# Four edits around the end of a kernel's first matrix product: who computes the last pair's moments, where its sums stand in the order, and when the weights' splitting begins

## The chip, the cores and the metric

The kernel runs on one core of a Trainium2 chip. The metric is the device time of one launch in microseconds (us), taken as the median of the runs shown. The kernel before took 2634.07 us (three runs, 2632.92 to 2637.14).

## What is computed

Two layers, each of a Fourier mixing step and a two-matrix network, over x with 2048 rows (S) and 576 columns (D); the network's inner width is 4608 (F).

```python
def _A_ref(x, dft_seq_re, dft_seq_im, dft_hid_re, dft_hid_im):
    a = jnp.einsum("bsd,ed->bse", x, dft_hid_re)
    b = jnp.einsum("bsd,ed->bse", x, dft_hid_im)
    return jnp.einsum("ts,bse->bte", dft_seq_re, a) - jnp.einsum("ts,bse->bte", dft_seq_im, b)

def _B_ref(x, w1, b1, w2, b2):
    y = _layernorm(x, axis=-1)
    h = _gelu(jnp.einsum("bsd,df->bsf", y, w1) + b1)
    return jnp.einsum("bsf,fd->bsd", h, w2) + b2

x = A_x
x = x + _A_ref(_layernorm(x), ...)
x = x + _B_ref(_layernorm(x), ...)
x = x + _A_ref(_layernorm(x), ...)
x = x + _B_ref(_layernorm(x), ...)
```

All data are float32.

## The kernel before

**Arithmetic.** A float32 product is made of three matmuls in a shorter format: each operand is split into a high part (ScalarE copies it into the rounded format) and a low part (VectorE subtracts the high part from the value), and TensorE adds high·high, high·low and low·high (`PASSES`). Most products also go through a scheme with seven instead of eight block products (numbers 1 to 7 in `ORDER`), so blocks are added and subtracted before they are split, and products are added to each other after (the "posts", done by VectorE, ScalarE and GpSimd).

**Stages of a layer.** First the sequence transform (class `Sequence`): it multiplies x, normalized, by the DFT matrix over rows. The 2048 rows are eight pairs (p = 0 to 7) of two 128-row tiles. Output tiles 0 and 1 (`PLAIN`) use plain products, pair by pair as the pairs come in (`first_mms`). Output tiles 2 to 15 use the seven products (`mms`), 24 matmuls each, so one output tile is 168 matmuls. Then follow, for each half of the rows, the hidden transform (`Hidden`, `hidden`) and the network (`mlp`). The network runs in groups g = 0 to 8 of two inner chunks q = 2g and 2g+1: an inner chunk is seven products of seven matmuls (49), each followed by a post, and between the chunks stand the second matrix's products of the group before (96 and 72 matmuls).

**The order of the work is written out by hand**: each engine does its instructions in the order in which the program issues them, and waits for what they need. Three orders matter here.

- `fill` prepares the pairs. For each pair: moments of the rows (`norm_stats`, which calls `stats_of_pair`), normalizing on ScalarE (`normalize`), high parts (`high_z`), low parts (`low_z`, VectorE), the sums of the seven-product scheme (`right_sums`: one subtraction on VectorE, then two on GpSimd, into the one buffer `t`), their high parts (`high_sums`, ScalarE) and low parts (`low_sums`, VectorE). At its end it also prepares the first left blocks of output tile 2: `low(*self.steps[0], True)` is the low part for product (2, 1) and, with it, three sums of the tile's blocks, `steps[1]` is product (2, 6), `steps[2]` is (2, 2). For pair p > 2 the four small steps behind the moments (L246, L247, L251, L252: add epsilon, power −1/2, multiply by the mean, negate) all stand on GpSimd.
- `run` walks the products n = 0, 1, ... (n = 0 to 6 is output tile 2): low part of product n+2, high part of n+3, the 24 matmuls, the post, and then two calls of `pump`.
- `pump` takes one step of `weights()`, a background generator that splits the network's first matrix into parts in DRAM, once for the whole program. It has 18 chunks of seven splits. It takes 4 steps for its first loads, one for the first high part, and two per split: the first makes the low part (VectorE, 128x384), a GpSimd sum if the split has one, and the next split's high part (ScalarE, L282 and L283); the second (`keep`) stores the split and loads a raw block for the next chunk. The last `keep` is step 257, and the last of chunk q is step 2·(7q + 6) + 7. A split lies in one of three buffers, so a high part waits until the store of three splits ago has landed. Pumps come from `run` (two per product, except product 2 of each tile: 84 of the 98 products, 168 pumps) and from the network's first half (12 per group from group 1 on, at the slots in `BEHIND`). If a chunk is wanted that isn't made yet, `load_w` pumps until it is (`while made[0] <= q`), in one go, at the place where it stands.

In the network, chunk q+1 is first wanted at the fourth product of chunk q (product 5), ahead of that product's matmuls and post. The post of product 5 is one VectorE addition that reads the bank into which product 3, two products on, adds; product 7 lies between.

Of the kernel before, what the change touches and what calls it, by code (L numbers as in the profile page):

```python
# [18 lines left out]
NP = NT // 2  # L19
# [139 lines left out]
def spectral_mixer(ctx: ExitStack, tc: tile.TileContext, x, dh, c0, cs, w1, b1, w2, b2, out):  # L159
# [35 lines left out]
    def add(engine, dst, a, b, op=OP.add):  # L195
        engine.tensor_tensor(dst, a, b, op=op)  # L196
# [65 lines left out]
    def weights():  # L262
        b = raw(4, 3 * P)
        a22, a21, a11, a12 = (b[:, k] for k in range(4))
        g = nc.gpsimd
        steps = ((4, a22, lambda: add(g, a22, a21, a22)), (1, a11, lambda: sub(g, a21, a11, a21)),
                 (5, a22, lambda: sub(g, a11, a22, a11)), (2, a12, lambda: sub(g, a12, a12, a11)),
                 (7, a21, None), (6, a11, None), (3, a12, None))

        def load(q, k):  # L270
            if q < NQ:
                dma(b[:, k], w1[q][:, k])

        def at(n):
            return stage(3, 5 * P)[:, n % 3]

        def cut(a):
            return a.rearrange("p (k f) -> p k f", f=P)

        def high(n):  # L280
            src, t = cut(steps[n % 7][1]), cut(at(n))
            nc.scalar.activation(t[:, 1:4:2], src[:, 0:3:2], AF.Copy)  # L282
            nc.scalar.activation(t[:, 2], src[:, 1], AF.Identity, bias=power[:, 2:3], scale=middle)  # L283

        def low(n):

            q, k = divmod(n, 7)
            i, src, then = steps[k]
            t = cut(at(n))
            sub(nc.vector, t[:, 0:5:2], cut(src), t[:, 1:4].bitcast(F32))  # L290
            if then:
                then()

        def keep(n):

            q, k = divmod(n, 7)
            stores[0].dma_start(w1s[q, steps[k][0] - 1], at(n).bitcast(F32))
            if k in (2, 4, 5, 6):
                load(q + 1, (2, 4, 5, 6).index(k))
            if k == 6:  # L300
                made[0] = q + 1

        for k in range(4):
            load(0, k)
        for _ in range(4):
            yield
        high(0)
        for n in range(7 * NQ):
            yield
            low(n)  # L310
            if n + 1 < 7 * NQ:
                high(n + 1)
            yield
            keep(n)
        stage.free()
        raw.free()
# [11 lines left out]
    class Sequence:  # L328
        def __init__(self, src, early):

            self.src, self.early = src, early
            self.Z, self.parts, self.b12, self.v, self.x, self.mv = [None] * NP, {}, {}, {}, {}, {}
            self.ready, self.closed, self.wish = 0, False, list(range(NP))
            self.normal, self.begun, self.xs, self.before = set(), {}, [], self.prepare()
            self.pieces = self.fill()


# [31 lines left out]
        def fill(self):  # L369
# [49 lines left out]
            for p in range(NP):  # L419
                if p in (1, 2) and self.early:  # L420
                    self.load_left(p + 1)
                if p + 1 < NP:
                    if p == 2 and self.early:
                        while self.closed:
                            yield
                        self.own.idle.insert(0, R.place(OWN_AT + 6 * NP * P + 2 * Z_N, 2 * NP * P))
                        sums, *self.xs = [A.alloc(2 * D, low=True) for _ in range(5)]
                    self.load_some()
                    while not self.has_z(p + 1):
                        yield  # L430
                if p == 1 and self.early:

                    self.high_sums(0)
                    self.low_left(1)
                    yield
                    self.low_sums(0)
                    yield
                    self.low_z(1)
                    yield
                    self.right_sums(1)  # L440
                    yield
                if p == 0 and not self.early:
                    self.half_stats(1)
                    self.low_z(0)
                    self.norm_stats(1)
                    self.low_left(0)
                    yield
                if p == 1 and not self.early:
                    self.low_left(1)
                if p + 1 < NP:  # L450
                    self.norm_stats(p + 1)
                if p == 0 and not self.early:
                    self.right_sums(0)
                    self.load_some()
                if p and (p != 1 or not self.early):
                    self.high_sums(p - 1)
                if p == 3 and self.early:

                    self.low_sums(p - 1)
                    self.t = sums  # L460
                    assert self.has_left(1)
                    for k in range(4, NP):
                        self.load_left(k)
                if p == 0 and self.early:
                    self.high_left(1)
                    self.high_z(1)
                elif p + 1 < NP:
                    self.high_parts(p + 1)
                yield
                if p > 1:  # L470
                    self.low_left(p)
                if p == 3:
                    self.begin_loads()
                if p == NP - 1:
                    self.idle += self.ring[4:]
                    self.high(PLAIN, 1)
                if p > 1 or p and not self.early:
                    yield
                    self.low_z(p)
                if p and (p not in (1, 3) or not self.early):  # L480
                    self.low_sums(p - 1)
                if p == NP - 1:
                    yield
                elif p > 1 or p and not self.early:
                    self.right_sums(p)
                    yield
            self.low(*self.steps[0], True)
            self.high(*self.steps[1])
            self.right_sums(NP - 1)
            self.high(*self.steps[2])  # L490
            self.high_sums(NP - 1)
            self.low(*self.steps[1])
            self.low_sums(NP - 1)
            yield
            for b in self.xs:
                if b.at != raw.at or self.early:
# [40 lines left out]
        def norm_stats(self, p):  # L537
            if p not in self.mv:
                halves = range(2 if p in self.begun else 0, 4)
                st, mv = self.begun.pop(p, None) or moments()  # L540
                measure(self.x[p], st, halves)
                self.mv[p] = stats_of_pair(st, mv, p == 0 and not self.early, p > 2, p == 1 and not self.early)

        def normalize(self, p):
            for h in range(2):
                at = slice(2 * h, 2 * h + 2)
                if p == 0 and not self.early:
                    v, mv = self.x[p][:, at], self.mv[p][:, h]
                    nc.vector.tensor_scalar(v, v, mv[:, 0:1], mv[:, 3:4], op0=OP.subtract, op1=OP.mult)
                    continue  # L550
                if p == 1 and not self.early:
                    shift(self.mv[p][:, h])
                normalize(self.x[p][:, at], self.x[p][:, at], self.mv[p][:, h])

# [168 lines left out]
        def run(self, hidden):  # L723
# [12 lines left out]
            for n, (t, i) in enumerate(steps):  # L736
                self.load_c()
                if n + 2 < len(steps):
                    self.low(*steps[n + 2])
                if i == 2 and t + 1 < NT:  # L740
                    self.sums(t + 1)
                self.load_c()
                if n + 3 < len(steps):
                    self.high(*steps[n + 3])
                self.mms(t, i)
                self.post(t, i)
                if n == 1:
                    self.first_turn(0, outs[0])
                    hidden.reserve()
                    self.first_post(1, outs[1])  # L750
                if n == 3:
                    self.first_turn(1, outs[1])
                if t == NT - 1:
                    hidden.begin(self, ORDER.index(i))
                if n == 3 and not self.early:
                    dma(b1t, b1)
                if n % 3 == 2 and 8 <= n < 8 + 3 * KH and not self.early:
                    dma(dhd[n // 3 - 2], dh[n // 3 - 2])
                if i != 2:
                    pump()  # L760
                    pump()
            for k in range(2):
# [709 lines left out]
```

## Time and profile before

| | us |
|---|---|
| median of three runs | 2634.07 |
| the profiled execution | 2634.11 |
| its span in the profile | 2632.3 |
| TensorE busy (99%) | 2617.2 |
| VectorE busy (70%) | 1834.1 |
| ScalarE busy (42%) | 1118.3 |
| GpSimd busy (30%) | 796.7 |

In the profile PE is TensorE's matmul, PEld its weight load, DVE VectorE, ACT ScalarE, POOL GpSimd and SP the engine that issues most DMAs. A group's line is that of the helper which issues it: L209 is every matmul, L196 an addition, L199 a subtraction (so low parts stand there, as R<-A,R), L667 the high part of a left block, L598 `high_sums`, L569 and L571 `high_z`, L256 `normalize`, L236 `shift`, L282 and L283 the high parts of a weights' split, L700 to L714 posts of the sequence transform. Times in a timeline are us from the start of the span; the number behind a group's x is how many instructions it merges; brackets give the engine's idle time before it and what ended it. Output tile 2 of the first layer runs from about 62 to 89 us, tile 3 to about 111 us, the first half of the first network from about 441 to 875 us, and the second layer's sequence transform from about 1300 us.

### The profile page before, as it was taken

Reading aid. Unit: us, or ns where it says so; the run is one execution under the profiler, and the core shown is the slowest. Engines: PE = TensorE matmul, PEld = TensorE weight load, DVE = VectorE, ACT = ScalarE, POOL = GpSimd, SP = SyncE. Lnnn points to the kernel's source line nnn. Section 1 sums busy time; section 2 is a strip of 40 time slices with the busy share of each in tenths; the row PEclk is TensorE's granted clock in tenths of the full one; section 3 lists DMA queues with packets and bytes.
Section 4 is the critical chain, followed back from the end, with each engine's and each line's share of the span. In section 5 each row is a group of like instructions: output and inputs, shape, how many; then the busy total and the mean of one; then the engine's idle time right before and its main releaser. Section 6 shows DMA issues by size and latency. Waiting matters only on the chain. (4 is left out here: it accounts for less than half of the span.)

```text
span 2632.3 us, 44772 instructions
## 1 busy us (share of the span) xinstructions
PE 2617.2 (99%) x17252; PEld 2466.4 (94%) x17252; DVE 1834.1 (70%) x2574; ACT 1118.3 (42%) x1815; POOL 796.7 (30%) x644
## 2 busy tenths in 40 slices
PE   9999999999999999999999999999999999999999
PEld 9999999899999989998999999999999999899998
DVE  8999987878777665556687776576555557655555
ACT  6555555555453443333354333353333325433332
POOL 6333433534444332222251000132222233322222
PEclk9999999999999999999999999999999999999999
DMA  5687786788788666677554333746666685666664
GB/s 184 226 273 241 244 259 215 262 276 286 275 286 299 184 194 195 195 222 212 170 177 132 124 123 124 210 153 192 195 195 195 195 274 157 200 195 194 194 195 156
DMA packets 223238, 544.91 MB, mean 207 GB/s; under 512 B 23712, under 2 KB 74912, under 8 KB 222880
## 3 DMA queue, kind: packets, MB, share of 16 engines
q1 hardware_dynamic: 209632, 511.94, 61.9%
q10 hardware_dynamic: 13392, 30.09, 3.0%
q8 instruction: 137, 2.24, 0.3%
q14 instruction: 77, 0.63, 0.1%
HBM read 429.87 MB, written 114.72 MB: 207 GB/s over the span
## 5 line engine op out<-in xcount | busy, mean ns | idle before, releaser
L209 PE MATMUL bank<-R 128*128 128x288 f32 (+2 forms) x16972 | 2587.4, 315 | 9.0 <-DVE R L199 3.8
L209 PEld LDWEIGHTS bank<-R 128*128 128x128 f32 x16972 | 2435.4, 189 | 157.0 <-DVE R L199 7.0
L196 DVE TENSOR_TENSOR A<-bank,A 128x576 f32<-128x576 f32 (+3 forms) x810 | 567.5, 708 | 520.2 <-PE bank L209 464.2
L199 POOL TENSOR_TENSOR R<-A,R 128x512 fp32r<-128x512 f32 (+1 forms) x290 | 376.0, 1305 | 909.6 <-ACT R L1261 548.7
L199 DVE TENSOR_TENSOR R<-A,R 128x1024 fp32r<-128x1024 f32 (+9 forms) x535 | 530.4, 1017 | 43.8 <-ACT R L667 12.5
L1261 ACT ACTIVATE R<-A 128x512 fp32r<-128x512 f32 x288 | 177.5, 630 | 355.7 <-DVE A L199 222.1
L196 POOL TENSOR_TENSOR A<-A 128x576 f32<-128x576 f32 (+2 forms) x102 | 156.2, 1536 | 539.5 <-ACT A L708 344.2
L1200 ACT ACTIVATE bank<-bank,b1t 128x512 f32<-128x512 f32 (+1 forms) x224 | 144.9, 647 | 360.9 <-DVE bank L196 235.8
L199 POOL TENSOR_TENSOR A<-A 128x288 f32<-128x288 f32 (+3 forms) x152 | 192.6, 1271 | 200.1 <-DVE R L199 95.3
L196 DVE TENSOR_TENSOR bank<-bank,A 128x512 f32<-128x512 f32 (+1 forms) x228 | 152.2, 669 | 143.5 <-PE bank L209 142.6
L667 ACT ACTIVATE R<-A 128x1024 fp32r<-128x1024 f32 x196 | 206.1, 1053 | 103.4 <-PE bank L209 60.2
L199 DVE TENSOR_TENSOR A<-A 128x1024 f32<-128x1024 f32 (+3 forms) x166 | 164.5, 996 | 6.2
L199 DVE TENSOR_TENSOR R<-bank,R 128x512 fp32r<-128x512 f32 x232 | 156.2, 676 | 4.3 <-ACT R L1261 3.7
L1261 ACT ACTIVATE R<-bank 128x512 fp32r<-128x512 f32 x216 | 121.1, 595 | 32.5 <-PE bank L209 32.5
L199 DVE TENSOR_TENSOR A<-bank,A 128x512 f32<-128x512 f32 x144 | 98.1, 681 | 0.4
L1227 ACT ACTIVATE A<-bank 128x512 f32<-128x512 f32 (+1 forms) x76 | 43.7, 575 | 120.2 <-PE bank L209 120.2
L282 ACT ACTIVATE R<-A 128x256 fp32r<-128x256 f32 x126 | 51.9, 412 | 64.0 <-DMA w_parts<-R 23.1
L1200 ACT ACTIVATE A<-bank,b1t 128x512 f32<-128x512 f32 (+1 forms) x76 | 50.5, 665 | 66.6 <-DVE bank L196 66.5
L230 POOL TENSOR_TENSOR moments<-moments,power 128x1 f32<-128x1 f32 x32 | 26.7, 834 | 129.8 <-DVE moments L232 112.0
L283 ACT ACTIVATE R<-A,power,middle 128x128 fp32r<-128x128 f32 x126 | 60.6, 481 | 0.0
L256 ACT ACTIVATE A<-A,moments 128x576 f32<-128x576 f32 x58 | 49.0, 866 | 23.5 <-POOL moments L252 13.6
L1135 ACT ACTIVATE R<-A 128x576 fp32r<-128x576 f32 x63 | 42.2, 676 | 15.8 <-DVE A L199 7.2
(65 smaller groups left out, 609.6 us busy)
## 6 DMA issues: line engine op xcount, KB each, us to landing
R<-w_parts SPq DMA_DIRECT2D x504, 320.0 KB, 3.4
R<-w_parts SPq DMA_DIRECT2D x189, 576.0 KB, 3.7
A<-in_cs SPq DMA_DIRECT2D x112, 512.0 KB, 4.5
w_parts<-R SPq DMA_DIRECT2D x63, 576.0 KB, 5.1
w_parts<-R ACTq DMA_DIRECT2D x81, 320.0 KB, 3.8
uv_mid<-A SPq DMA_DIRECT2D x28, 576.0 KB, 5.4
w_parts<-R SPq DMA_DIRECT2D x45, 320.0 KB, 4.5
A<-in_w SPq DMA_DIRECT2D x72, 192.0 KB, 4.9
```

The costliest lines, as they stand in the source:

```text
L196: engine.tensor_tensor(dst, a, b, op=op)
L199: engine.tensor_tensor(dst, a, b, op=OP.subtract)
L209: nc.tensor.matmul(o, a, b, start=start, stop=stop, skip_group_check=True)
L230: nc.gpsimd.tensor_tensor(mv[:, 3:4], mv[:, 2:3], power[:, 0:1], op=OP.pow)
L256: nc.scalar.activation(dst, src, AF.Identity, bias=mv[:, 4:5], scale=mv[:, 3:4])
L282: nc.scalar.activation(t[:, 1:4:2], src[:, 0:3:2], AF.Copy)
L283: nc.scalar.activation(t[:, 2], src[:, 1], AF.Identity, bias=power[:, 2:3], scale=middle)
L667: nc.scalar.activation(self.cells[t, i](2, NP, P)[:, 0], self.source(t, i), AF.Copy)
L1135: nc.scalar.activation(got2[g, i](2, 2, DH)[:, :, 0], src, AF.Copy)
L1200: nc.scalar.activation(dst, src, AF.Gelu_apprx_tanh, bias=bias(f))
L1227: nc.scalar.activation(up, o, AF.Copy)
L1261: nc.scalar.activation(H[q, k](2, TC)[:, 0], src, AF.Copy)
```

## The change

1. **Moments of the last pair** (p = 7, both layers): L246 goes to VectorE, and instead of the two GpSimd steps L251 and L252, VectorE negates the mean (L249) and ScalarE multiplies it (`shift`, L236, once for each half). GpSimd keeps the power.
2. **Sums of the last pair** (both layers): `right_sums(7)` moves ahead of the low part of product (2, 1) and the three sums behind it; `high_sums(7)` moves ahead of the high parts of products (2, 6) and (2, 2); `low_sums(7)` moves ahead of the low part of (2, 6).
3. **Pumps**: no pumps at products n = 0 to 6, so the first output tile with seven products has no step of `weights()`. All later ones come 12 pumps later in the program.
4. **Order of the splits**: products 6 and 7 change places within a chunk, and with them which raw block is loaded at which `keep` (block 2 one split earlier, block 1 one split later).

```diff
-                 (7, a21, None), (6, a11, None), (3, a12, None))
+                 (6, a11, None), (7, a21, None), (3, a12, None))
...
             if k in (2, 4, 5, 6):
-                load(q + 1, (2, 4, 5, 6).index(k))
+                load(q + 1, {2: 0, 4: 2, 5: 1, 6: 3}[k])
...
+            self.quick = (NP - 1,) if early else (1, NP - 1)
...
+            self.right_sums(NP - 1)
             self.low(*self.steps[0], True)
+            self.high_sums(NP - 1)
             self.high(*self.steps[1])
-            self.right_sums(NP - 1)
             self.high(*self.steps[2])
-            self.high_sums(NP - 1)
+            self.low_sums(NP - 1)
             self.low(*self.steps[1])
-            self.low_sums(NP - 1)
...
-                self.mv[p] = stats_of_pair(st, mv, p == 0 and not self.early, p > 2, p == 1 and not self.early)
+                self.mv[p] = stats_of_pair(st, mv, p == 0 and not self.early, 2 < p < NP - 1, p in self.quick)
...
-                if p == 1 and not self.early:
+                if p in self.quick:
                     shift(self.mv[p][:, h])
...
-                if i != 2:
+                if i != 2 and n >= 7:
                     pump()
                     pump()
```

Three places show how instructions move. The first is VectorE at the end of `fill` in the first layer, from the low part of the sums of pair 6. Before (3x288 and 4x288 are pairs, 1024 left blocks, A<-A 2x288 is `right_sums`):

```order
L199 TENSOR_TENSOR R<-A,R 128x4x288
L199 TENSOR_TENSOR R<-A,R 128x1024
L196 TENSOR_TENSOR A<-A 128x1024
L199 TENSOR_TENSOR A<-A 128x1024 x2
L199 TENSOR_TENSOR A<-A 128x2x288
L199 TENSOR_TENSOR R<-A,R 128x1024
L199 TENSOR_TENSOR R<-A,R 128x4x288
L199 TENSOR_TENSOR R<-A,R 128x1024
```

And now:

```order
L199 TENSOR_TENSOR R<-A,R 128x4x288
L199 TENSOR_TENSOR A<-A 128x2x288
L199 TENSOR_TENSOR R<-A,R 128x1024
L196 TENSOR_TENSOR A<-A 128x1024
L199 TENSOR_TENSOR A<-A 128x1024 x2
L199 TENSOR_TENSOR R<-A,R 128x4x288
L199 TENSOR_TENSOR R<-A,R 128x1024 x2
```

The subtraction of `right_sums` moved up four places, and the low part of its sums, which stood behind the low part of (2, 6), now stands before it.

The second place is VectorE in the network's group 7, second inner chunk (q = 15), about the post of product 5. Before:

```order
L196 TENSOR_TENSOR A<-bank,A 128x512
L199 TENSOR_TENSOR R<-A,R 128x2x288
L199 TENSOR_TENSOR R<-A,R 128x3x128
L196 TENSOR_TENSOR A<-bank,A 128x512
L199 TENSOR_TENSOR R<-A,R 128x2x288
```

And now:

```order
L196 TENSOR_TENSOR A<-bank,A 128x512
L199 TENSOR_TENSOR R<-A,R 128x2x288
L199 TENSOR_TENSOR R<-A,R 128x3x128 x4
L196 TENSOR_TENSOR A<-bank,A 128x512
L199 TENSOR_TENSOR R<-A,R 128x2x288
```

The first `A<-bank,A 128x512` is the post of product 6, the second that of product 5; between them stood one low part of a weights' split (3x128), and now four.

The third is the same place in group 8, first inner chunk (q = 16). Before:

```order
L196 TENSOR_TENSOR A<-bank,A 128x512
L199 TENSOR_TENSOR R<-A,R 128x2x288
L199 TENSOR_TENSOR R<-A,R 128x3x128 x2
L196 TENSOR_TENSOR A<-bank,A 128x512
L199 TENSOR_TENSOR R<-A,R 128x2x288
```

And now:

```order
L196 TENSOR_TENSOR A<-bank,A 128x512
L199 TENSOR_TENSOR R<-A,R 128x2x288
L199 TENSOR_TENSOR R<-A,R 128x3x128 x5
L196 TENSOR_TENSOR A<-bank,A 128x512
L199 TENSOR_TENSOR R<-A,R 128x2x288
```

There two low parts became five.

## The prediction

> **What bounds the kernel now.** I read the page's busy table first.
>
> ```profile
> span 2632.3 us, 44772 instructions
> PE 2617.2 (99%) x17252; PEld 2466.4 (94%) x17252; DVE 1834.1 (70%) x2574; ACT 1118.3 (42%) x1815; POOL 796.7 (30%) x644
> ```
>
> TensorE sets the time: all its idle time together is 15 us. An edit to other engines can only win back stalls of PE or add new ones. So I looked for the stalls in the stretches that the change touches, first by windows (span; then PE, PEld, DVE, ACT, POOL busy; clock; DMA share; GB/s).
>
> ```profile
> 40.00:145.00 105.00, 101.41 (x749) 99.30 (x748) 95.51 (x102) 62.65 (x106) 41.38 (x34) 1.00 0.53 181
> 150.00:375.00 225.00, 225.00 (x1704) 225.00 (x1703) 209.51 (x212) 130.53 (x236) 87.92 (x56) 1.00 0.75 249
> 1360.00:1390.00 30.00, 29.28 (x217) 28.58 (x216) 25.89 (x28) 18.30 (x28) 10.05 (x9) 1.00 0.14 42
> ```
>
> From 150 to 375 us PE never waits: 225/1704 = 0.132 us a matmul, at full clock, with DVE 93% busy. At that pace 40 to 145 us would hold 795 matmuls and holds 749, so 46 x 0.132 = 6.1 us are lost there. The second layer's 30 us would hold 227 and hold 217: 1.4 us. The timeline of PE says where (start, length, count, idle before).
>
> ```profile
> 49.75 5.59 PE L209 MATMUL bank<-R 128*128 128x288 f32 x41
> 55.76 13.23 PE L209 MATMUL bank<-R 128*128 128x288 f32 x97 [0.42 <-DVE R L199]
> 69.33 12.73 PE L209 MATMUL bank<-R 128*128 128x288 f32 x94 [0.34 <-DVE R L199]
> 82.50 6.91 PE L209 MATMUL bank<-R 128*128 128x288 f32 x50 [0.43 <-ACT A L708]
> 90.32 23.21 PE L209 MATMUL bank<-R 128*128 128x288 f32 x168 [0.91 <-DVE R L199]
> 114.76 25.68 PE L209 MATMUL bank<-R 128*128 128x288 f32 x190 [1.24 <-DVE R L199]
> 140.60 9.69 PE L209 MATMUL bank<-R 128*128 128x288 f32 x71 [0.16 <-ACT A L700]
> ```
>
> From one start to the next, less 0.132 us a matmul, the losses are 0.60 (up to 55.76), 0.77 (69.33), 0.76 (82.50), 1.22 (90.32), 2.26 (114.76) and 0.76 (140.60), 6.4 us in all; a little is matmul records that are missing, so I scale to the window's 6.1: 1.4 for the first two, 4.7 for the other four. Nearly all are VectorE's low parts that come late.
>
> **Edits 1 and 2: the last pair.** The stall at 55.76 is `low_z(7)`. Its chain, in the timelines of POOL, ACT and DVE, and from the groups of ACT the price of a `shift`:
>
> ```profile
> 48.70 1.37 POOL L247 TENSOR_TENSOR moments<-moments,power 128x2 f32<-128x2 f32 x1
> 52.08 2.55 POOL L199 TENSOR_TENSOR A<-A 128x288 f32<-128x288 f32 x2
> 49.57 1.04 ACT L557 ACTIVATE R<-A 128x1024 fp32r<-128x1024 f32 x1
> 52.02 1.63 ACT L256 ACTIVATE A<-A,moments 128x576 f32<-128x576 f32 x2 [1.40 <-POOL moments L252]
> 53.69 0.93 ACT L569 ACTIVATE R<-A 128x864 fp32r<-128x864 f32 x1
> L236 ACT ACTIVATE moments<-moments,power 128x1 f32<-128x1 f32 x2 | 0.8, 380 | 2.5 <-POOL moments L247 2.5
> 54.64 3.88 DVE L199 TENSOR_TENSOR R<-A,R 128x864 fp32r<-128x864 f32 x4 [1.58 <-ACT R L569]
> 58.44 1.22 DVE L196 TENSOR_TENSOR A<-A 128x1024 f32<-128x1024 f32 x1
> 59.69 3.15 DVE L199 TENSOR_TENSOR A<-A 128x1024 f32<-128x1024 f32 x3
> 63.30 1.58 DVE L199 TENSOR_TENSOR R<-A,R 128x1024 fp32r<-128x1024 f32 x1 [0.46 <-ACT R L667]
> 66.79 2.49 DVE L199 TENSOR_TENSOR R<-A,R 128x1152 fp32r<-128x1152 f32 x2 [1.90 <-ACT R L598]
> ```
>
> The power now ends before 50.1, and ACT is free at 50.6. Two shifts at 0.38 and the normalizing (1.63) put `high_z` at 53.05 instead of 53.69: DVE starts 0.64 earlier, at 54.0, and the stall of 0.6 goes. The two small VectorE steps that replace L246 and L251 cost 0.2 us each at most, ahead of the waits of DVE. `right_sums(6)` on POOL (52.08, two at about 1.28) waits for VectorE's subtraction, not for the moments, so `high_sums(6)` and `low_sums(6)` stay and still end at about 57.3 (the third of the four in the 54.64 row).
>
> From 57.3 on, VectorE now does: subtraction of `right_sums(7)` 0.7, low (2, 1) 1.14, the sum 1.25, two subtractions 2.4, `low_sums(7)` 1.27, low (2, 6) 1.22: 65.3. Before, low (2, 6) stood ahead of `low_sums(7)` and ended at 64.9. Now there is something else: the two POOL instructions of `right_sums(7)` run while VectorE works without a break. What this costs was seen at 85 us:
>
> ```profile
> 84.26 4.92 POOL L199 TENSOR_TENSOR A<-A 128x288 f32<-128x288 f32 x3
> 85.29 1.71 DVE L199 TENSOR_TENSOR A<-A 128x1024 f32<-128x1024 f32 x1
> 69.31 1.23 DVE L199 TENSOR_TENSOR A<-A 128x1024 f32<-128x1024 f32 x1
> ```
>
> The same VectorE subtraction took 1.71 beside POOL's and 1.23 alone, and POOL's took 1.64 instead of 1.28. Twice 0.5 gives low (2, 6) at 66.4. PE without the stall would want it 74 matmuls behind 55.1, at 64.9: a new stall of 1.5, with 0.15 for the restart 1.65. So the first layer loses 1.65 where it lost 1.4. The second layer has the same orders and steps; its three stalls make 1.4 to 1.5, the first goes and the rest is about as large as now: nothing. **Together +0.3.** Bounds: all of the stalls go, -2.8; or the first stall stays since `low_z(7)` meets `right_sums(6)` on POOL (+0.6) and the second layer has the new stall in full (+1.0), +1.9. I take the value near the middle since each step has a row.
>
> [...]
>
> **Edits 3 and 4: no pumps in tile 2.** The stalls from 82.50 on (4.7) lie behind the first weights' steps: at 82.50 the post L708 stood behind high parts on ACT, 90.32 is VectorE still behind, and 114.76 is this wait of ACT, for the raw block of the next split, with the sequence's own high part queued behind it:
>
> ```profile
> 110.99 0.42 ACT L282 ACTIVATE R<-A 128x256 fp32r<-128x256 f32 x1 [6.69 <-DMA A<-in_w]
> ```
>
> With the steps one tile later, VectorE has some 15 low parts less to do while it still catches up with the fill. The swap of products 6 and 7 lets block 2, for which ACT waited, be loaded 5 pumps ahead of its high part instead of 3; what comes nearer is block 1, whose GpSimd sum now stands 3 pumps behind its load, but its high part two more. The steady stretch has all these steps at the same rate with no stall, so I let 4.2 of 4.7 go and keep the first post's delay. Bounds: all 4.7; or the beginning itself recurs one tile on (0.7 + 1.5 for ACT's wait + 0.4) and only 2.1 go. **-4.2.**
>
> The pumps that fall away come back elsewhere. The sequence now gives 156 instead of 168, and a network group gives 12. Chunk 16 (243 steps) is wanted in group 7 when 156 + 6 x 12 + 9 = 237 are done: `load_w` takes 6 at once. Chunk 17 (257) is wanted in group 8 when 156 + 84 + 6 + 3 = 249 are done: 8 at once. Before, the same count gave 249 (none missing) and 255 (2 missing). The low parts of these bursts stand on VectorE ahead of the post of product 5, and PE may not go on to product 3 until that post has read its bank. What a burst of two did, and where the posts are now (DVE's, ACT's and PEld's timelines about both places):
>
> ```profile
> 769.18 0.41 ACT L282 ACTIVATE R<-A 128x256 fp32r<-128x256 f32 x1
> 769.49 0.48 ACT L283 ACTIVATE R<-A,power,middle 128x128 fp32r<-128x128 f32 x1
> 771.82 0.70 DVE L196 TENSOR_TENSOR bank<-bank,A 128x512 f32<-128x512 f32 x1 [0.26 <-PE bank L209]
> 772.43 0.55 DVE L199 TENSOR_TENSOR R<-A,R 128x384 fp32r<-128x384 f32 x1
> 791.86 0.68 DVE L196 TENSOR_TENSOR A<-bank,A 128x512 f32<-128x512 f32 x1
> 792.59 4.47 PEld L209 LDWEIGHTS bank<-R 128*128 128x128 f32 x23 [0.38 <-DVE A L196]
> DMA to landing us min/median/max: 2.7/2.7/2.7
> DMA to landing us min/median/max: 2.2/2.5/2.8
> DMA to landing us min/median/max: 2.2/4.5/7.5
> ```
>
> The last three rows are the stores of splits (L297): the one issued at 768.9, the two at 791.5 and 792.0, and all 45 from 440 to 830 us. With only one more low part in its way the post came at 791.86 to 792.54, and PE lost 0.3. A low part waits for its high part (ACT, 0.79 for the pair), which waits until the store of three splits ago has landed. Group 7: three more low parts; the last high part needs the store of 768.9 (landed 771.6), then 0.79, the low part and the post: 772.9 to 773.6, where PE wants product 3 at 771.7: **+2.0** with the restart. Group 8: the fourth high part needs the store of the burst's own first low part, issued 791.5; landed 794.2 (2.7), high 795.0, low 795.6, with the hops between engines post 796.1 to 796.8, where PE wants it at 792.4: 4.4, with the restart 4.55, less the 0.3 lost before: **+4.3**. Together **+6.3.** Bounds: if no store is waited for, ACT's pace alone (0.79 a low part) makes 1.4 and 2.0: +3.4. If the stores land as the median of all, 4.5, each burst loses 1.8 more, +9.9, and with a raw block that isn't there in time (1 us) +11. I take 2.7, since it was measured at these two places.
>
> [...]
>
> **The sum.** -4.2 + 0.3 + 6.3 = +2.4 on the profiled execution's 2634.11, which is the median of the runs (2634.07) to 0.04: **2636.5 us**. This kernel can be told from no change beyond about 0.2%, 5.3 us: below 2628.8 is faster, above 2639.3 slower.
>
> **The rivals.**
> - *Stores land late in the bursts* (slower). The burst sends its stores within about 2 us of each other beside the loads of the second matrix, and the median of all stores is 4.5. Then +9.9 for the bursts: 2634.1 - 4.2 + 0.3 + 9.9 = **2640.1**. It decides from a landing of about 4.1 us on (two waits x 1.45 = 2.9 more than the forecast). Against it: 2.2 to 2.8 at these very places.
> - *The bursts are hidden.* PE would find product 3's bank free in time. For it: in group 7 the stores before the burst are over 2 us old, so that only its last high part waits. Against it: even a burst of two cost 0.3. Then -4.2 + 0.3 = **2630.2**.
> - *The beginning only moves a tile on*, so that the change doesn't do what it is made to: -2.1 instead of -4.2. For it: VectorE is full in tile 3 too. Against it: the steady stretch. **2638.6**, with the bursts as forecast.
> - *Everything comes off*, stalls of both layers and bursts hidden: -4.7 - 2.8 = **2626.6**.
>
> **How the numbers follow.** Forecast 0.50, late stores 0.20, the beginning moved 0.12, bursts hidden 0.11, everything 0.07. The forecast's own range is 2632.5 to 2640: its terms' middle bounds. The range that should hold 8 in 10 is 2629.5 to 2642: it takes in the hidden bursts, the moved beginning and most of the late stores, and leaves out everything coming off and the latest landings. Slower: the late stores (0.16 of their 0.20 lie above 2639.3), a third of the moved beginning, and a tail of the forecast of 0.05: 0.25. Faster: everything, and a fourth of the hidden bursts: 0.10. Within 0.2%: 0.65.
>
> **What the changed kernel's profile would show.** Edit 1: ACT's normalizing of the last pair starts by 51.1 and the PE gap at 55.8 is gone. Edit 2: VectorE's instructions from 57 to 62 us at 1.6 to 1.7 instead of 1.2, and a PE gap at about 65 to 66 of 1.5; wrong if VectorE shows 1.2 or PE no gap. Edits 3 and 4: no gaps at 82 and 90 us, no wait of ACT for a raw block of over 2 us in 100 to 140. Bursts: PE gaps of about 2 us near 772 and of 4.5 near 793, ended by VectorE's L196, with L282 on ACT ended by a store; wrong if these gaps are under 1 us, and the price is wrong if the stores there land later than 4 us.

## The result

The changed kernel took 2641.55 us (median of seven, 2638.59 to 2645.69) against 2634.07 (seven, 2632.84 to 2637.14). The ratio is 1.0027, 95% interval 1.0018 to 1.0037: slower, by 7.5 us where +2.4 was forecast. The direction held, and so did the wide range (2629.5 to 2642), by 0.45 us. The result lies above the forecast's own range (2632.5 to 2640) and above 2639.3, from where on the prediction called the kernel slower, with a chance of 0.25.

The profiled execution took 2645.69 us with a span of 2643.9, 11.6 more than the span before and 4 us above its own median, so some of what it shows does not happen in every execution. The windows of the changed kernel that answer to those shown before (columns as there):

```profile
40.00:145.00 105.00, 103.07 (x775) 102.44 (x775) 94.88 (x102) 61.35 (x99) 35.47 (x27) 1.00 0.51 168
150.00:375.00 225.00, 223.30 (x1679) 222.00 (x1678) 212.67 (x208) 128.92 (x231) 83.25 (x56) 1.00 0.73 244
1360.00:1390.00 30.00, 28.06 (x208) 27.39 (x208) 28.11 (x38) 20.88 (x29) 15.89 (x13) 1.00 0.27 100
```

The fill and the first tiles hold 26 matmuls more than before (775 for 749): that part of the change works. But the stretch that had no stall has lost 25 (1679 for 1704), and the second layer's 30 us have lost 9. PE's timeline names the new gaps:

```profile
66.61 0.53 PE L209 MATMUL bank<-R 128*128 128x288 f32 x2 [1.15 <-ACT R L668]
67.92 92.33 PE L209 MATMUL bank<-R 128*128 128x288 f32 x696 [0.78 <-DVE R L199]
774.32 21.13 PE L209 MATMUL bank<-R 128*128 128x512 f32 x121 [1.49 <-DVE A L196]
799.18 31.10 PE L209 MATMUL bank<-R 128*128 128x512 f32 x174 [3.73 <-DVE A L196]
1388.56 0.53 PE L209 MATMUL bank<-R 128*128 128x288 f32 x2 [1.16 <-ACT R L668]
1389.87 5.38 PE L209 MATMUL bank<-R 128*128 128x288 f32 x27 [0.79 <-DVE R L199]
```

The table adds up, for every matmul of a stretch, the time from its start to the next start less the usual time of its shape (0.132 us for 288 columns, 0.23 for 512), where that is over 0.03 us. This catches gaps, restarts and slow stretches alike.

| stretch, us | lost before | lost after | difference | forecast |
|---|---|---|---|---|
| 40 to 145 | 6.05 | 2.66 | -3.4 | -3.9 |
| 145 to 400 | 1.15 | 4.64 | +3.5 | 0 |
| 400 to 500 | 3.42 | 4.08 | +0.7 | 0 |
| 750 to 850 (bursts) | 1.22 | 8.36 | +7.1 | +6.3 |
| 1350 to 1400 (second layer) | 1.53 | 5.21 | +3.7 | 0 |
| sum | | | +11.6 | +2.4 |

Three things are new against the prediction. The first is the granted clock (the last column but two) behind some of the gaps:

```profile
68.20:71.00 2.80, 2.80 (x23) 2.80 (x23) 2.77 (x3) 1.50 (x3) 0.00 (x0) 1.00 0.02 6
800.00:804.00 4.00, 4.00 (x12) 3.16 (x11) 1.10 (x2) 1.35 (x2) 2.71 (x2) 0.58 0.99 314
1390.50:1394.00 3.50, 3.50 (x17) 3.50 (x16) 2.81 (x3) 1.14 (x2) 0.00 (x0) 0.52 0.18 37
```

Behind the 3.7 us gap, and behind the pair of gaps in the second layer, TensorE ran at half clock for 3.41 us (799.91 to 803.32 and 1390.42 to 1393.83): it stays busy, with a matmul each 0.43 us for 0.23 and each 0.24 for 0.132, and the span grows by another 1.5 us each time. Behind the same pair of gaps in the first layer the clock stayed at 1.00 (the first row).

The second is the price of edits 1 and 2, in the timelines of POOL, DVE and ACT in the first layer:

```profile
52.73 3.46 POOL L199 TENSOR_TENSOR A<-A 128x288 f32<-128x288 f32 x2 [3.00 <-DVE A L199]
54.47 2.04 DVE L199 TENSOR_TENSOR R<-A,R 128x864 fp32r<-128x864 f32 x2 [0.74 <-ACT R L570]
57.42 1.36 DVE L199 TENSOR_TENSOR R<-A,R 128x1152 fp32r<-128x1152 f32 x1 [0.91 <-ACT R L599]
60.63 1.83 DVE L196 TENSOR_TENSOR A<-A 128x1024 f32<-128x1024 f32 x1
62.49 2.97 DVE L199 TENSOR_TENSOR A<-A 128x1024 f32<-128x1024 f32 x2
65.50 2.95 ACT L668 ACTIVATE R<-A 128x1024 fp32r<-128x1024 f32 x3 [1.17 <-DVE A L199]
```

The sums of pair 6 on GpSimd take 3.46 us, where they took 2.55; `low_sums(6)` ends at 58.8 instead of 57.3; VectorE's next sums run at 1.83 and 1.49 instead of 1.23; and the high part of product (2, 6) on ScalarE, which needs those sums, starts at 65.5 instead of 62.2, after PE wanted it (0.5 us of these delays is the execution's own, whose fill is that much later in all its parts). The forecast had this gap, but only one of it (1.65), for the low part.

The third is the loss between 145 and 400 us, with its gaps at 246, 276, 318 and 385 (part of the last, 0.9 us between 380 and 400, was lost before too). It needed the experiments.

### The profile page after: what moved, and what is told of

Read it like the earlier page. It is cut to its first block, busy times and chain, and to the rows that moved or that the text cites. A ratio compares the mean times of both kernels' runs of the same rounds, so it can differ in the third digit from the quotient of the medians.

```text
span 2643.9 us, 44764 instructions
## 1 busy us (share of the span) xinstructions
PE 2619.9 (99%) x17252; PEld 2467.7 (93%) x17252; DVE 1841.9 (70%) x2578; ACT 1120.6 (42%) x1819; POOL 788.1 (30%) x638
## 5 line engine op out<-in xcount | busy, mean ns | idle before, releaser
L196 DVE TENSOR_TENSOR A<-bank,A 128x576 f32<-128x576 f32 (+3 forms) x810 | 567.9, 708 | 522.4 <-PE bank L209 481.2
L199 POOL TENSOR_TENSOR R<-A,R 128x512 fp32r<-128x512 f32 (+1 forms) x290 | 376.2, 1305 | 903.8 <-ACT R L1262 536.9
L199 DVE TENSOR_TENSOR R<-A,R 128x1024 fp32r<-128x1024 f32 (+9 forms) x535 | 538.8, 1031 | 46.2 <-ACT R L668 13.0
L196 POOL TENSOR_TENSOR A<-A 128x576 f32<-128x576 f32 (+2 forms) x102 | 151.4, 1489 | 582.6 <-ACT A L709 347.0
L668 ACT ACTIVATE R<-A 128x1024 fp32r<-128x1024 f32 x196 | 206.0, 1054 | 117.5 <-PE bank L209 66.3
L196 DVE TENSOR_TENSOR bank<-bank,A 128x512 f32<-128x512 f32 (+1 forms) x228 | 152.4, 670 | 144.4 <-PE bank L209 143.4
L199 POOL TENSOR_TENSOR A<-A 128x288 f32<-128x288 f32 (+3 forms) x152 | 194.5, 1283 | 177.9 <-DVE R L199 81.7
L199 DVE TENSOR_TENSOR A<-A 128x1024 f32<-128x1024 f32 (+3 forms) x166 | 163.2, 987 | 6.3
L199 DVE TENSOR_TENSOR R<-bank,R 128x512 fp32r<-128x512 f32 x232 | 156.4, 677 | 4.3 <-ACT R L1262 3.7
L199 DVE TENSOR_TENSOR A<-bank,A 128x512 f32<-128x512 f32 x144 | 98.3, 683 | 0.4
```

Of the source, the lines that this page charges most:

```text
L199: engine.tensor_tensor(dst, a, b, op=OP.subtract)
L668: nc.scalar.activation(self.cells[t, i](2, NP, P)[:, 0], self.source(t, i), AF.Copy)
```

## The experiments

All times are compared with runs of the kernel before on the same chip (the third column has their median); the last column counts the executions whose mean granted clock was below 1.000. One stretch of 3.4 us at half clock lowers that mean by 0.0006.

| kernel | us | before, us | ratio and interval | clock below 1.000 |
|---|---|---|---|---|
| edit 1 | 2635.82 | 2634.40 | 1.0007 (0.9998 to 1.0016) | 1 of 11 |
| edit 2 | 2632.42 | 2634.40 | 0.9994 (0.9985 to 1.0003) | 0 of 11 |
| edits 1, 2 | 2635.79 | 2635.60 | 1.0005 (0.9995 to 1.0014) | 10 of 11 |
| edit 3 | 2640.07 | 2634.40 | 1.0024 (1.0015 to 1.0033) | 11 of 11 |
| edit 3, more pumps | 2632.13 | 2634.91 | 0.9987 (0.9978 to 0.9996) | 0 of 11 |
| edit 4 | 2633.72 | 2634.87 | 0.9996 (0.9987 to 1.0005) | 0 of 11 |
| edits 1, 2, 3 | 2645.73 | 2634.91 | 1.0034 (1.0022 to 1.0047) | 5 of 5 |
| all four | 2641.55 | 2634.07 | 1.0027 (1.0018 to 1.0037) | 7 of 7 |
| all four, more pumps | 2636.45 | 2634.40 | 1.0008 (0.9999 to 1.0017) | 6 of 11 |
| edits 2, 3, more pumps | 2632.37 | 2634.87 | 0.9989 (0.9981 to 0.9998) | 0 of 11 |
| edit 2, sums of pair 7 on VectorE | 2632.31 | 2634.87 | 0.9990 (0.9981 to 0.9999) | 1 of 11 |
| edits 1, 2, sums of pairs 6, 7 on VectorE | 2631.24 | 2634.87 | 0.9988 (0.9979 to 0.9996) | 2 of 11 |
| the same, edit 3, more pumps | 2632.05 | 2634.91 | 0.9987 (0.9978 to 0.9996) | 0 of 11 |

**Edit 3 alone.**

```diff
-                if i != 2:
+                if i != 2 and n >= 7:
```

> Edit 3 alone (no pumps in output tile 2). My account of the changed kernel: the stalls from 82 to 145 us go (-4.5), and the two bursts in groups 7 and 8 come (+5.8, and up to +1.6 more where TensorE's granted clock is halved behind the longer stall): +1 to +3 us against the kernel before, with PE gaps of about 1.6 and 3.9 us near 772 and 795 us. Rival: the loss lies in the fill (edits 1 and 2) and the bursts only hide what would be lost anyway: -4 us.

It lost 5.7 us by the medians, more than the 1 to 3 expected: the account, with a larger price. Both bursts stand in PE's timeline, and the clock is halved behind the second (797 to 800 us):

```profile
69.02 63.73 PE L209 MATMUL bank<-R 128*128 128x288 f32 x480 [0.34 <-DVE R L199]
133.51 48.07 PE L209 MATMUL bank<-R 128*128 128x288 f32 x358 [0.77 <-DVE R L199]
182.09 18.16 PE L209 MATMUL bank<-R 128*128 128x288 f32 x135 [0.51 <-ACT A L700]
770.91 21.49 PE L209 MATMUL bank<-R 128*128 128x512 f32 x121 [1.48 <-DVE A L196]
796.53 6.66 PE L209 MATMUL bank<-R 128*128 128x512 f32 x26 [4.13 <-DVE A L196]
797.00:800.00 3.00, 3.00 (x9) 2.35 (x8) 1.02 (x3) 0.66 (x1) 2.72 (x2) 0.50 1.01 310
```

The stalls from 82 to 145 us are gone, but two came in their place, at 134 and 182 (with restarts and small ones 2.1 us): here the beginning of the splits did move a tile on in part, as one rival had it. One more price of edit 3 was in no account: a PE gap of 0.5 to 0.8 us near 485 us, ended by GpSimd's L199, stands in all seven traces with edit 3 and in none without.

**Edit 3 without its bursts.** Fourteen pumps in each network group, two of them in the outer parts (slots 9 and 22):

```diff
-BEHIND = (0, 2, 2, 4, 5, 6, 15, 17, 17, 19, 21, 21)
+BEHIND = (0, 2, 2, 4, 5, 6, 9, 15, 17, 17, 19, 21, 21, 22)
```

> Edit 3 alone with 14 pumps in each network group (added at slots 9 and 22), so with no burst: what the pumps' absence from tile 2 is worth by itself. My account: the gaps from 82 to 145 us go, two of about 1 us come at 134 and 182: -2.5 from 50 to 200 us, at most 1 back in the network: 2632 to 2633.5, 7 us under edit 3 alone. Rival (the prediction's): the whole 4.2 comes off: 2630 to 2631.

2632.13, 2.8 under before, and PE has no gap where the bursts were:

```profile
759.82 45.45 PE L209 MATMUL bank<-R 128*128 128x288 f32 x269
```

With the run above this prices the bursts at 8.5 us by the medians; the two traces differ by 8.0 between 750 and 850 us. Edit 3 by itself is worth some 3 us, where the prediction had 4.2 for it and edit 4.

**Edit 2 alone, edit 1 alone.** The order of the end of `fill`, and the moments of pair 7:

```diff
+            self.right_sums(NP - 1)
             self.low(*self.steps[0], True)
+            self.high_sums(NP - 1)
             self.high(*self.steps[1])
-            self.right_sums(NP - 1)
             self.high(*self.steps[2])
-            self.high_sums(NP - 1)
+            self.low_sums(NP - 1)
             self.low(*self.steps[1])
-            self.low_sums(NP - 1)
```

```diff
-                self.mv[p] = stats_of_pair(st, mv, p == 0 and not self.early, p > 2, p == 1 and not self.early)
+                self.mv[p] = stats_of_pair(st, mv, p == 0 and not self.early, 2 < p < NP - 1, p in self.quick)
-                if p == 1 and not self.early:
+                if p in self.quick:
                     shift(self.mv[p][:, h])
```

> Edit 2 alone (sums of the last pair ahead of the left blocks). My account: the high part of product (2, 6) now waits for sums of the left blocks that VectorE makes 3 us later, and VectorE and GpSimd lock each other out: two new PE gaps near 66 and 68 us, about 1.4 and 1.0, in place of the ones near 68 and 69 us (0.7), in both layers: +2 to +5 us. Rival: the order gains, and what was lost there came from the moments of edit 1: -1 to -2 us.

> Edit 1 alone (moments of the last pair mostly off GpSimd). My account: the PE gap near 55.8 us goes in both layers, the later ones stay: -1 us (-1.4 to 0). Rival: the steps on VectorE delay right_sums(6) and with it low_sums(6), and the gap comes back a little later: 0 to +1 us.

Both came out on the side of the rival. Edit 2 took 2 us off (the interval just includes none), edit 1 added 1.4 (likewise), which is more than its rival's 0 to 1. DVE's and PE's timelines with edit 2 alone:

```profile
54.41 2.75 DVE L199 TENSOR_TENSOR R<-A,R 128x864 fp32r<-128x864 f32 x3 [1.58 <-ACT R L569]
59.00 1.83 DVE L196 TENSOR_TENSOR A<-A 128x1024 f32<-128x1024 f32 x1
60.86 2.98 DVE L199 TENSOR_TENSOR A<-A 128x1024 f32<-128x1024 f32 x2
63.76 3.62 DVE L199 TENSOR_TENSOR R<-A,R 128x1152 fp32r<-128x1152 f32 x3
66.30 33.88 PE L209 MATMUL bank<-R 128*128 128x288 f32 x250 [0.78 <-DVE R L199]
```

One gap at 66.3, with low (2, 6) ready there: the prediction's 66.4 and its cause, VectorE's sums at 1.83 and 1.49. What it missed stands in the same block: low (2, 2) follows at once and ends at 67.4, where it ended at 69.3, and with VectorE that much ahead the stalls at 82 and 90 us do not come at all: 250 matmuls without a gap, although tile 2 still has its pumps. These stalls belonged to the backlog of the fill as much as to the pumps. With edit 1 alone (POOL, DVE, PE):

```profile
53.06 3.47 POOL L199 TENSOR_TENSOR A<-A 128x288 f32<-128x288 f32 x2 [2.99 <-DVE A L199]
57.77 2.50 DVE L199 TENSOR_TENSOR R<-A,R 128x1152 fp32r<-128x1152 f32 x2 [0.92 <-ACT R L599]
66.67 2.95 PE L209 MATMUL bank<-R 128*128 128x288 f32 x20 [0.61 <-DVE R L199]
```

`high_z(7)` is earlier and the gap near 55.8 is gone, but `low_z(7)` now runs while GpSimd is still at the sums of pair 6, which take 3.47 instead of 2.55; `low_sums(6)` starts only at 57.77 (some 0.8 us of this is the execution's own, late before pair 7's moments begin; VectorE's two added steps make the beginning of the sums 0.2 later, the rest is their length) and everything behind it is late: 2.05 us of gaps up to 72 us where there were 1.4, and 2.6 instead of 1.5 in the second layer.

**Edits 1 and 2 together.**

> Edits 1 and 2 together, alone. Alone, edit 2 measured 2632.4 and edit 1 2635.8, against 2634.4. My account: together they don't add, since low_sums(6) is late (edit 1) ahead of the longer chain to product (2, 6) (edit 2): two PE gaps near 66 and 68 us, 1.4 and 1.05, in both layers, and, as they lie within 3 us, in a part of the executions a halved clock behind them, 1.5 to 1.8 us a layer: 2635.5 to 2639, with executions apart by steps of about 1.6 us. Rival: the effects add: 2633.5 to 2634.2.

2635.79: neither the sum of the two (-0.6) nor the best of them. Ten of eleven executions had a clock below 1.000, and the times lie from 2632.16 (the one at 1.000) to 2640.53. That two gaps within 3 us halve the clock was the expectation's estimate, and no run shows such a limit: the pairs here (1.16 and 0.79 us in the first layer, 0.45 and 0.78 in the second) have 0.53 us of work between them. In the profiled execution the pair of gaps in the first layer is followed by half clock, and the one in the second is not (1.00 from 1380 to 1386 us):

```profile
68.20:71.00 2.80, 2.80 (x13) 2.80 (x13) 2.77 (x3) 1.11 (x2) 0.00 (x0) 0.50 0.03 6
```

13 matmuls where the changed kernel had 23 in the same 2.8 us behind the same two gaps.

**Does GpSimd hold VectorE up?** The two GpSimd subtractions of `right_sums` on VectorE, for pair 7 with edit 2 (the same with `NP - 1`), and for pairs 6 and 7 with edits 1 and 2:

```diff
-            sub(nc.gpsimd, t[:, 1], v[:, 2], t[:, 0])
-            sub(nc.gpsimd, t[:, 3], v[:, 3], t[:, 1])
+            e = nc.vector if p >= NP - 2 else nc.gpsimd
+            sub(e, t[:, 1], v[:, 2], t[:, 0])
+            sub(e, t[:, 3], v[:, 3], t[:, 1])
```

> Edit 2 alone, and the two GpSimd subtractions of the last pair's sums done by VectorE too. If the two engines lock each other out, VectorE's 1024-wide sums near 60 us take 1.22 again instead of 1.83 and 1.49, which about pays for the two added steps (0.45 each): the gap near 66 us stays within 0.3 us of its 1.0, time 2631.5 to 2633.5. Rival: the long sums have another cause (a DMA, the transposes) and stay long: the gap grows to 1.9, +1 us a layer, 2634 to 2635.

> Edits 1 and 2, and the GpSimd subtractions of the last two pairs' sums done by VectorE. If edit 1 lost because pair 6's sums on GpSimd now meet low_z(7) on VectorE, low_sums(6) is no longer late, the gap near 55.8 us is gone and the one near 66 us is 1.2 to 1.5: about -0.3 us a layer against edit 2 alone, 2631 to 2632.5. Rival: edit 1 loses by its own steps on VectorE and ScalarE: 2634 or more.

Both as the account had them by which the two engines lengthen each other's instructions (2632.31 and 2631.24). DVE of the first, where only the two subtractions of pair 7 differ from edit 2 alone:

```profile
57.51 1.75 DVE L199 TENSOR_TENSOR A<-A 128x576 f32<-128x576 f32 x3
60.31 1.22 DVE L196 TENSOR_TENSOR A<-A 128x1024 f32<-128x1024 f32 x1
61.56 2.48 DVE L199 TENSOR_TENSOR A<-A 128x1024 f32<-128x1024 f32 x2
```

DVE and PE of the second:

```profile
59.78 1.22 DVE L196 TENSOR_TENSOR A<-A 128x1024 f32<-128x1024 f32 x1
61.03 2.49 DVE L199 TENSOR_TENSOR A<-A 128x1024 f32<-128x1024 f32 x2
65.98 34.28 PE L209 MATMUL bank<-R 128*128 128x288 f32 x253 [0.66 <-DVE R L199]
```

The same sums take 1.22 and 1.25 again, so VectorE does two more steps (about 0.5 each) in no more time; the gap at 55.8 is gone without a price, and one of 0.93 is left at 66. In the traces the second loses about 0.6 us less in the fill and 0.5 less in the second layer than the first, but by their times the two cannot be told apart, and pair 6's sums were not tried on VectorE without edit 1, so that edit 1 pays in this form is not shown. VectorE's sum took 1.83 beside GpSimd's subtractions and 1.22 without them, and GpSimd's two subtractions 3.41 beside it where they took 2.56 before. That the two "lock each other out", as the expectations put it, is an account of this; the rows show the lengths alone.

**Edit 4 alone, and the three others without it.** The order of the splits and loads:

```diff
-                 (7, a21, None), (6, a11, None), (3, a12, None))
+                 (6, a11, None), (7, a21, None), (3, a12, None))
-                load(q + 1, (2, 4, 5, 6).index(k))
+                load(q + 1, {2: 0, 4: 2, 5: 1, 6: 3}[k])
```

> Edit 4 alone (order of the splits and of their raw loads). My account: ACT's long wait for a raw block near 111 us and the PE gap behind it (1.5) go, but the raw block whose load now stands one split later is late for GpSimd's sum, and with it ACT's high part and the sequence's own posts and high parts behind it: GpSimd waits for raw loads, and PE gaps of 2 to 3.5 us in all between 200 and 350 us: +0.5 to +2 us. Rival: those gaps came from the shifted pumps, not from this order: -1.5 us and none of these gaps.

> Edits 1, 2 and 3 without edit 4. My account: the gaps between 240 and 350 us of the changed kernel (3.3) go, the bursts and their halved clock, and the two gaps of the sums (1.4 and 1.05 a layer), stay; the beginning of the splits leaves two gaps of about 1 us near 134 and 182 us: 2 us under the changed kernel, 2638.5 to 2640. Rival: those gaps come from the later pumps: 2641 to 2642, and the gaps stand.

The gaps came and went with edit 4, as expected: with it alone ACT's wait near 111 us is gone with 2.0 of the 2.2 us lost between 100 and 150, and 2.4 us are lost between 200 and 300 us, with PE's gaps at these places:

```profile
224.75 35.81 PE L209 MATMUL bank<-R 128*128 128x288 f32 x264 [0.26 <-DVE R L199]
260.73 22.51 PE L209 MATMUL bank<-R 128*128 128x288 f32 x168 [0.17 <-DVE R L199]
283.82 16.44 PE L209 MATMUL bank<-R 128*128 128x288 f32 x122 [0.58 <-DVE R L199]
```

Without it, in the other run, PE has no gap from 185.4 to 345 us. The time of edit 4 alone did not come as expected: it was to be 0.5 to 2 us above before, and 2633.72 lies 1.2 below, with an interval that includes none, so edit 4 alone cannot be told from no change. The waits of ACT and POOL in 200 to 345 us point to the link, before and then with all four edits (us in total, times, longest):

```profile
ACT R L282 <- POOL A L196: 2.1, 2, 1.9
```

```profile
ACT R L282 <- POOL A L196: 10.6, 5, 3.5
POOL A L196 <- DMA A<-in_w: 14.1, 1, 14.1
```

The raw block that is now loaded one split later goes into GpSimd's sum, and ScalarE's high part waits for that sum, with the sequence's own posts behind it. With edit 4 alone the first of these waits adds up to 7.5 us, with the three other edits to 4.3, so it comes mainly with edit 4. That the late load makes the sum late is seen once with all four edits, in the wait of 14.1 us that a load ended (before, no load ended such a wait in this stretch); with edit 4 alone the profile puts GpSimd's waits there down to other engines, and for them it is argued. The time of edits 1 to 3 was a miss: 2645.73 where 2638.5 to 2640 was expected. Its profiled execution has half clock in three places, after the pairs of gaps of both layers and around the second burst (at 799 to 800 us, still in the gap, and 800.8 to 805):

```profile
68.20:71.00 2.80, 2.80 (x13) 2.80 (x13) 2.77 (x3) 1.23 (x2) 0.00 (x0) 0.50 0.03 6
800.80:805.00 4.20, 4.20 (x11) 3.27 (x10) 1.29 (x2) 1.35 (x2) 2.78 (x2) 0.50 0.99 323
1392.50:1396.00 3.50, 3.50 (x17) 3.50 (x17) 2.23 (x2) 0.52 (x1) 0.00 (x0) 0.52 0.25 88
```

Its two executions with a mean clock of 0.999 took 2641.8 and 2642.9, the three with 0.997 or 0.998 took 2645.7 to 2647.0. The rest of the miss is not explained. Nor do the medians add: edits 1 and 2 (+0.2), edit 3 (+5.7) and edit 4 (-1.2) make 4.7 where the change took 7.5. Intervals of some 2.4 us each way leave open whether that difference is real.

**The change without bursts, and the candidates.** All four edits with two added pumps a group, at slots 9 and 12 of the first outer part:

```diff
+BEHIND = (0, 2, 2, 4, 5, 6, 9, 12, 15, 17, 17, 19, 21, 21)
```

> All four edits, with two more pumps in each network group (14 for 12, at the two added slots 9 and 12 of its first outer part), so that no burst is left. My account: the gaps near 774 and 799 us go with the halved clock behind them: -6 to -7.5 us against the changed kernel, so 2634 to 2636, about as before. Rival: the added pumps cost as much on VectorE in the seven groups as the bursts did: 2640 to 2642.

2636.45, just above the expected 2634 to 2636: 5 us come back, less than the bursts' 7.1, and what stays is mainly the two pairs of gaps, half clock behind the first of them (0.51 from 67.6 to 71 us), edit 4's 2.5 us, and a new loss of 0.27 us in each group, where an outer part ends. With slot 22 in place of 12 that is gone in most groups. Edits 2 and 3, and then edits 1 to 3 with the sums of pairs 6 and 7 on VectorE:

> Edits 2 and 3 with 14 pumps in each network group (added at slot 9 of the first outer part and slot 22, the beginning of the second; not at slot 12). My account: edit 2's gain of 1.8 stays, edit 3 saves some 1 to 2.5 of what is left of the gaps from 82 to 145 us, no burst, and the PE gap of 0.27 a group that came with slot 12 is gone: 2630 to 2632. Rival: the added low parts delay a post wherever they stand: 2633 or more.

> Edits 1 and 2 with the subtractions of the last two pairs' sums on VectorE, and edit 3 with 14 pumps a group: the candidate. My account: from the kernel without edit 3 (-3.6 us against before) the gaps near 95 to 139 us (2.8) go, 2 come back at 134 and 182, up to 1 in the network: within 1 us of it, 2630 to 2632. Rival: with the fill's backlog gone the later beginning leaves nothing: 2628 to 2629.5.

2632.37 and 2632.05, both just above the expected 2630 to 2632. Once edit 2 has removed VectorE's backlog, edit 3 finds little to win. Five versions lie 0.10 to 0.13% under the kernel before with intervals below 1, and cannot be told apart; the lowest median is that of edits 1 and 2 with the last two pairs' sums on VectorE.

## Why the prediction was right in direction, and where its sizes failed

- **The range held in part by luck.** Its slow side was there for stores that land late in the bursts (2640.1), and they did not. What filled it were losses that the sum had at nothing: the second layer's (+3.7 in the profiled execution), the steady stretch's (+3.5) and the clock's.
- **The count of the pumps** (6 and 8 forced, in groups 7 and 8) and the mechanism held: gaps in front of product 3, ended by VectorE's L196, and in the second burst a high part that waits for a store (in the first none did; there ScalarE's own pace was enough). The gaps were 1.75 and 4.0 us with their restarts for 2.0 and 4.55; the stores of the second burst landed in 2.2 to 2.5, where 2.7 was taken, so the rival of late stores was not what made the time longer. DVE, ACT and the stores of the second burst:

```profile
796.27 0.42 ACT L282 ACTIVATE R<-A 128x256 fp32r<-128x256 f32 x1 [1.36 <-DMA w_parts<-R]
797.97 0.56 DVE L199 TENSOR_TENSOR R<-A,R 128x384 fp32r<-128x384 f32 x1 [0.31 <-ACT R L283]
798.44 0.69 DVE L196 TENSOR_TENSOR A<-bank,A 128x512 f32<-128x512 f32 x1
DMA to landing us min/median/max: 2.2/2.2/2.5
```

- **The term that was missing there** is the clock: +1.6 us of half clock behind the second burst, and by the mean clock in every execution of edit 3 alone. The sum took a gap to cost its own length and at most 0.15 for the restart, a term that no row shows: behind the gaps of 0.42 to 3.73 us in the traces before and after, the restart of matmuls of 288 and 512 columns cost 0.23 to 0.28.
- **"`right_sums(6)` waits for VectorE's subtraction, not for the moments, so `high_sums(6)` and `low_sums(6)` stay"** was the step that failed in edit 1. The beginning stayed to 0.2 us, the duration did not: an earlier `low_z(7)` runs into it. The lengthening that the prediction priced for pair 7 (1.71 for 1.23 on VectorE, 1.64 for 1.28 on GpSimd) was overlooked for pair 6 (3.46 for 2.55 on GpSimd).
- **One gap of 1.65 a layer for edits 1 and 2** became two (1.4 and 1.05), since the high part of (2, 6) is late too. That came from `low_sums(6)`, as edit 2 alone has one gap only. "The second layer: nothing" missed 1 us of gaps and the half clock, 1.5 us in a part of the executions; the rest of the 3.7 is mainly a gap at 1358 us in the profiled execution (0.9 with its restart), whose cause stays open. For edit 2 alone the sum would have been too dark: that the next low part comes earlier was not counted.
- **-4.2 for edits 3 and 4** was the steady stretch taken as proof that the same steps do no harm one tile later. Edit 3 alone left 2.1 at 134 and 182 us. With edit 4 these are gone and the stretch from 40 to 145 us is nearly as good as forecast (-3.4 for -3.9), but the steady stretch itself loses 3.5: the load that "comes nearer" for GpSimd's sum was named and priced at nothing.

## What to carry to other kernels

Work that runs in the background on a count of steps must be counted to its end: taking steps away early makes a burst where the count is due, and two more steps a group cost next to nothing at slots 9 and 22, and 0.27 us a group with slot 12. A step that starts earlier beside GpSimd can finish the rest later (edit 1 alone: 2.05 us of gaps up to 72 us for 1.4), so price what it runs into, not only what it waited for. And two short gaps of TensorE close to each other can cost more than their length (1.16 and 0.79 us in the changed kernel's second layer, with 3.41 us at half clock behind them).

## What was not expected of the hardware

The granted clock fell to 0.50 around the end of the second burst's gap, in all three profiled executions with such a gap: for 3.41 us from 799.91 us, behind 3.73 us, in the changed kernel; at 797 to 800 us, behind 4.13 us, with edit 3 alone; and at 799 to 800, still in the gap, and 800.8 to 805 us with edits 1 to 3. It fell to 0.50 behind pairs of gaps too (in the timelines 1.15 or 1.16, once 0.45, and then 0.78 or 0.79 us, with 0.53 us of work between them), at five of the seven places whose clock is shown: behind both pairs with edits 1 to 3, behind the second layer's in the changed kernel, behind the first layer's with edits 1 and 2 and with all four edits and more pumps; it stayed at 1.00 behind the first layer's in the changed kernel and the second layer's with edits 1 and 2. Behind the single gaps of up to 1.49 us in the traces before and after it stayed at 1.00. Why the same pair of gaps does it in one layer and not in the other is not shown. Nor is it shown that the clock makes the times vary: those of edits 1 and 2 lie 8.4 us apart (2632.16 to 2640.53), those with the sums of pairs 6 and 7 on VectorE, whose trace has no such pair, 8.9 (2628.91 to 2637.80).

GpSimd's small steps were short where VectorE was idle: there the four moments steps of a pair, two elements a partition, took 0.19 to 0.71 us, and 1.19, 1.37, 1.04 and 0.72 beside VectorE's low parts and (the last) its subtraction, for the last pair of the first layer before. In the changed kernel's second layer, POOL's four moments steps of a pair:

```profile
1354.04 0.22 POOL L246 TENSOR_SCALAR moments<-moments 128x2 f32<-128x2 f32 x1
1354.34 0.71 POOL L247 TENSOR_TENSOR moments<-moments,power 128x2 f32<-128x2 f32 x1
1355.13 0.19 POOL L251 TENSOR_TENSOR moments<-moments 128x2 f32<-128x2 f32 x1
1355.40 0.20 POOL L252 TENSOR_TENSOR moments<-power,moments 128x2 f32<-128x2 f32 x1
```

So part of the time that edit 1 set out to move off GpSimd came with VectorE's work beside it; whether it was waiting or slower work is not shown. The power, which it left there, took 1.66 instead of 1.37.
